# Attention, routed experts and a dense layer on one core: the routing's lists and re-ranking are issued a step at a time

## The chip, the core and the metric

One Trainium2 chip, one of its cores. The time is device microseconds of one execution of the whole program. Before the change three runs took 1547.67, 1550.4 and 1554.59 us; the median is 1550.4 us. A separate, profiled execution took 1545.65 us.

## What is computed

```python
# attention, per head: 32 packed queries p attend to k, v; then q attends to the packed result
p_packed = softmax(p k^T / 8) v
x = softmax(q p_packed^T / 8) p_packed            # 4608 tokens x 512
# routed experts: all 4608 x 8 scores in falling order
for idx in argsort(-(x @ w_gate).flatten()):
    tok, e = idx // 8, idx % 8
    if assigned[tok] >= 0 or counts[e] >= 576: continue
    assigned[tok] = e; counts[e] += 1
for e in range(8):
    out[assigned == e] = relu(x[assigned == e] @ w1[e]) @ w2[e]
# dense layer: 512 -> 2048 -> 512
h = out @ w_in;  result = (h * tanh(softplus(h))) @ w_out
```

Each expert ends with exactly 576 tokens.

## The kernel before

The program has three stretches. Attention comes first; its last part writes the token rows `x` to DRAM (`px`). Then the experts: for each, 192 products "up" (`pm<-xh,w` and `pm<-xl,w`, results `h`) and 192 "down" (`pm<-h,w`, results `y`), 288 columns each; a float32 product is made of three, of high and low parts of both sides. Then the dense layer (`ph`, `po`).

The routing (class `Routing`) runs beside the experts' products. It doesn't sort: it finds the experts one after the other in the order in which they fill up (0 to 7 here, in that order). For each, `search` finds the threshold score in seven digits. A digit is a chain: VectorE compares all tokens with the steps (`ge`, line 359), PE counts (line 367), VectorE copies the counts (`sb`, 372), PE adds them up (376), VectorE compares with the places left (`ind`, 380), PE spreads the answer (383), VectorE takes the digit over (`dg`, `at`, 387 to 390). `accept` marks the tokens of the found expert (`be`, `run`), re-ranks what is left (`rank`, lines 319 to 340: the best open score of each token as `m`, `ev`, `am`, `oh`, `key`, `first`), and PE counts places in line 435, called "total" here. `ids` then builds the expert's list of tokens on VectorE (`p0`, `pi`, `pif`, `oj`, `rj`, `oh`, lines 449 to 466), PE gathers it (470, 478), and `idx` is the list.

PE's order is written by hand. `Turns` counts one turn per product; a generator that yields n is resumed n turns later. The routing, the `fetch` of the next expert and the decoding of the dense layer's 64-bit weights (`Decode.step`, tiles `dt`, `dbig`) are such generators. How many turns each waits stands in the table `WAITS`, by expert 0, expert 1 and all later ones. The other engines' instructions are put in order by the scheduler; only those passed through `keep_in_program_order` stay in the written order against each other.

`fetch(k)` waits until expert k is found, loads the expert's number from `ei` on SyncE's queue, and asks for weights: each of eight loads is a DMA to `raw`, a cast on ScalarE (`w<-raw`, 513) and four subtractions of 256 columns on GpSimd (`w<-raw,w`, 516), here called splits. There are ten weight tiles, so those of the next expert come as the running one gives its tiles back. Then `gather` fetches the token rows on GpSimd's DMA queue (`xg`, 619), and PE transposes them (`pt`, 630) for `xh` (ScalarE) and `xl` (VectorE).

```python
    def __call__(self, n=1, idle=False):     # Turns: one call per product
        for s in list(self.streams):
            if idle and not s[2]: continue
            s[1] -= n
            while s[1] <= 0:
                wait = next(s[0], None)
```

Of the kernel before, what the change touches and what calls it, by code (L numbers as in the profile page):

```python
# [244 lines left out]
class Routing:  # L245
# [7 lines left out]
    def __init__(self, tc, a, consts, wk, ident, idx_all):  # L253
# [8 lines left out]
        self.code, self.pcode = rc[:, 128:136], rc[0:8, 136:137]  # L262
        self.tri = T([128, 128], BF, "tri")
# [55 lines left out]
    def rank(self):  # L319

        nc, V, T, L = self.nc, self.nc.vector, self.tile, self.L

        def bc(ap):
            return ap[:, :, None].to_broadcast([128, 36, NE])

        m = T([128, 36], F32, "m")
        V.tensor_reduce(m, L, axis=AX.X, op=OP.max)
        ev = T([128, 36, NE], F32, "ev", 1)
        V.tensor_tensor(ev, L, bc(m), op=OP.is_equal)
        key = self.key = T([128, 36], I32, "key")  # L330
        bits = m.bitcast(I32)
        V.tensor_scalar(key, bits, 31, -0x80000000, op0=OP.arith_shift_right, op1=OP.bitwise_or)
# [3 lines left out]
        V.tensor_mul(ev, ev, self.code[:, None, :].to_broadcast([128, 36, NE]))  # L336
        am = self.next_am = T([128, 36], F32, "am")
        V.tensor_reduce(am, ev, axis=AX.X, op=OP.max)
        self.oh = T([128, 36, NE], F16, "oh8", 1)
        V.tensor_tensor(self.oh, ev, bc(am), op=OP.is_equal)  # L340

    def search(self, k):
# [57 lines left out]
        V.tensor_scalar(self.ei[0:1, k:k + 1], a[0:1], -1.0, float(NE), op0=OP.mult, op1=OP.add)  # L400
        V.tensor_add(self.closed, self.closed, a)
        r = T([8, 3], F32, "r")
        V.scalar_tensor_tensor(sc[0:8, 0:n - 1], pc[0:8, 1:n], 1.0, dg[0:8, 0:n - 1], op0=OP.mult, op1=OP.mult,
                               accum_out=r[:, 0:1])
        V.tensor_tensor(r[:, 1:2], self.rem, r[:, 0:1], op=OP.subtract)
        V.tensor_scalar(r[:, 2:3], self.pcode, a[0:8], float(NT), op0=OP.is_equal, op1=OP.mult)
        V.tensor_tensor(self.rem, r[:, 1:2], r[:, 2:3], op=OP.max)
        cl = T([128, NE], F32, "cl")
        V.tensor_scalar(cl, self.code, a, -BIG, op0=OP.is_equal, op1=OP.mult)
        V.tensor_add(L, L, cl[:, None, :].to_broadcast([128, 36, NE]))  # L410

    def accept(self, k):
        nc, V, T, q = self.nc, self.nc.vector, self.tile, self.q
        t, a = q[:, 0:1], q[:, 1:2]
        z = T([128, 4, 36], F32, "z")
# [15 lines left out]
        if k < NE - 2:  # L431
            self.rank()
        yield wait(k, "total")
# [9 lines left out]
        self.slot = z[:, 2]  # L443

    def ids(self, k, slot):
        nc, V, T = self.nc, self.nc.vector, self.tile
        p0 = T([128, 36], I32, "p0", 1)
        self.tc.keep_in_program_order(
            V.tensor_scalar(p0, slot, 0.5, -32.0 * WIDE, op0=OP.is_lt, op1=OP.mult))
        V.scalar_tensor_tensor(p0, slot, 64.0 * (k % 2) - 1.0, p0, op0=OP.add, op1=OP.add)  # L450
        pi = T([128, 2, 36], I32, "pi", 1)
        V.tensor_scalar(pi[:, 1], p0, 5, None, op0=OP.arith_shift_right)
        V.tensor_scalar(pi[:, 0], p0, 31, None, op0=OP.bitwise_and)
        pif = T([128, 2, 36], BF, "pif", 1)
        V.tensor_copy(pif, pi)
# [4 lines left out]
        oj = T([128, 9, 20, 4], BF, "oj", 1)  # L460
        V.tensor_tensor(oj, spread(pif[:, 1], 20), self.steps[:, :, 0:20], op=OP.is_equal)
        rj = T([128, 2, 9, 20, 4], BF, "rj", 1)
        for h in range(2):
            V.tensor_tensor(rj[:, h], oj, spread(self.parts[:, h], 20), op=OP.mult)  # L464
        oh = T([128, 9, 32, 4], BF, "oh", 1)
        V.tensor_tensor(oh, spread(pif[:, 0], 32), self.steps[:, :, 0:32], op=OP.is_equal)
# [25 lines left out]
    def phases(self, turns):  # L492
        for k in range(NE):
            yield from self.search(k)
            self.found = k
            yield from self.accept(k)
            while k and k - 1 not in self.idx:
                yield 1
            turns.add(self.ids(k, self.slot))
# [265 lines left out]
def fused_kernel(ctx: ExitStack, tc: tile.TileContext, a: dict, out: bass.AP):  # L765
# [38 lines left out]
    with tc.manual_schedule(engines={mybir.EngineType.PE}):  # L804
# [12 lines left out]
        def fetch(k):  # L817
            while rt.found < k:
                yield 1
            w = ex.weights(k)  # L820
            for _ in range(4):
                next(w)
            while k not in rt.idx:
                yield 1
            yield from ex.gather(k, rt.idx[k], w)

        def decode():
            for i in range(32):
                yield DECODE - 6 * DECODE_OP
                yield from dec.step(words(i), i // 2, i % 2)  # L830
# [98 lines left out]
```

## Time and profile before

| what | before |
|---|---|
| median of 3 runs | 1550.4 us (1547.67 to 1554.59) |
| profiled execution: its time / its span | 1545.65 us / 1543.9 us |
| PE busy | 1447.7 us, 94% of the span |
| VectorE (DVE) / ScalarE (ACT) / GpSimd (POOL) busy | 821.6 / 783.2 / 417.9 us |
| first "up" product of expert 0, last "down" of expert 7 | 190.14, 741.72 us |

The profile has one page and a trace that answers questions. A view of windows gives each engine's busy time in a stretch, with the TensorE clock that was granted there as a share of 2.4 GHz. A view of waits names who waited for whom. A timeline lists instructions in order of time. Line numbers are those of the listing.

### The profile page before, as it was taken

What the parts mean: (1) busy time and instruction counts of PE and PEld (TensorE: products, weight loads), DVE (VectorE), ACT (ScalarE), POOL (GpSimd) and SP (SyncE); (2) the same over time, 40 slices, a digit from 0 to 9 for tenths busy, and PEclk for the clock granted to TensorE, in tenths of its full rate; (3) what the DMA queues carried; (4) which work ended last, traced back from release to release, by engine and by line L of the source; (5) the groups of instructions that cost most, each with busy time, mean ns of one, the idle gap of its engine ahead of it and who ended that gap; (6) DMA issues with size and microseconds to landing.
All of it is one profiled execution on the core that took longest, in us unless ns stands there. A gap on an engine that the chain in (4) does not pass through costs nothing.

```text
span 1543.9 us, 22783 instructions
## 1 busy us (share of the span) xinstructions
PE 1447.7 (94%) x9009; PEld 1195.1 (77%) x9009; DVE 821.6 (53%) x1632; ACT 783.2 (51%) x966; POOL 417.9 (27%) x572
## 2 busy tenths in 40 slices
PE   6879698898979899999999999999999999999997
PEld 3335487787879798999888888888888888888885
DVE  4765576757586776432344454444444444444443
ACT  2334443433333344544656565666656565656564
POOL 2441355546454647742601010010101000010101
PEclk9998798998989999999999999999999999999999
DMA  9743636345444556742502020100102010100000
GB/s 344 289 140 137 212 128 212 135 158 169 151 143 170 167 178 210 267 159 100 181 1 81 1 82 0 55 28 25 58 1 82 1 55 28 55 29 0 28 0 28
DMA packets 66843, 165.38 MB, mean 107 GB/s; under 512 B 8880, under 2 KB 21808, under 8 KB 66736
## 3 DMA queue, kind: packets, MB, share of 16 engines
q1 hardware_dynamic: 60656, 144.00, 27.1%
q0 software_dynamic: 6080, 19.93, 3.9%
q8 instruction: 71, 1.16, 0.3%
q14 instruction: 36, 0.29, 0.1%
HBM read 117.76 MB, written 46.14 MB: 106 GB/s over the span
## 4 chain that ended last, share of the span: by engine, by line
issue 48%; PE 32%; DVE 10%; POOL 5%; DMA 3%; ACT 1%; SPq 0%; POOLq 0%; ACTq 0%
PE pm L592 21%; PE px L238 3%; PE po L734 2%; PE ph L592 2%; POOL w L211 2%; POOL w L516 2%; POOL out L744 2%; DMA raw<-in_w 1%; PE pt L630 1%; DVE h L656 1%; DVE rj L464 1%; DVE w L180 1%; PE pr L376 1%; PE pr L367 1%; PE big L108 1%
## 5 line engine op out<-in xcount | busy, mean ns | idle before, releaser
L592 PE MATMUL ph<-y,w 128*128 128x512 f32 x1728 | 414.9, 395 | 0.0
L734 PE MATMUL po<-w,g 128*128 128x512 f32 x1728 | 410.1, 394 | 0.1
L592 PEld LDWEIGHTS ph<-y,w 128*128 128x128 f32 x1728 | 324.2, 188 | 78.1
L734 PEld LDWEIGHTS po<-w,g 128*128 128x128 f32 x1728 | 324.9, 188 | 74.6 <-ACT g L709 0.9
L709 ACT ACTIVATE u<-u 128x1024 f32<-128x1024 f32 (+1 forms) x219 | 229.4, 1049 | 194.4 <-DVE u L713 192.8
L516 POOL TENSOR_TENSOR w<-raw,w 128x256 fp32r<-128x256 f32 x320 | 248.2, 812 | 130.0 <-ACT w L513 92.3
L592 PE MATMUL pm<-h,w 128*128 128x288 f32 x1536 | 240.3, 307 | 1.4 <-DVE h L656 1.4
L592 PE MATMUL pm<-xh,w 128*128 128x288 f32 x1024 | 225.3, 309 | 13.6 <-DVE h L656 12.9
L744 POOL DMA_INDIRECT out<-ot,idx_all x36 | 35.0, 973 | 726.7 <-DVE ot L742 720.9
L592 PEld LDWEIGHTS pm<-h,w 128*128 128x128 f32 x1536 | 214.0, 193 | 6.2 <-DVE h L656 1.8
L713 DVE TENSOR_SCALAR u<-ph 128x1024 f32<-128x1024 f32 (+1 forms) x73 | 88.2, 1210 | 201.2 <-PE ph L592 201.2
L592 PEld LDWEIGHTS pm<-xh,w 128*128 128x128 f32 x1024 | 173.5, 196 | 17.4 <-DVE h L656 14.3
L709 ACT ACT_TABLE_LOAD x144 | 184.8, 1283 | 2.5
L716 DVE TENSOR_TENSOR u<-ph,u 128x1024 f32<-128x1024 f32 (+1 forms) x73 | 88.2, 1210 | 172.6 <-ACT u L709 172.6
L592 PE MATMUL pm<-xl,w 128*128 128x288 f32 x512 | 157.7, 308 | 0.1
L709 ACT ACTIVATE g<-u 128x1024 fp32r<-128x1024 f32 (+1 forms) x73 | 76.4, 1048 | 101.3 <-DVE u L718 101.3
L718 DVE TENSOR_TENSOR u<-ph,u 128x1024 f32<-128x1024 f32 (+1 forms) x73 | 88.1, 1208 | 73.2 <-ACT u L709 73.2
L513 ACT ACTIVATE w<-raw 128x1024 fp32r<-128x1024 f32 x80 | 84.1, 1056 | 62.9 <-DMA raw<-in_w 45.7
L655 ACT ACTIVATE h<-pm 128x288 fp32r<-128x288 f32 x128 | 51.5, 408 | 118.1 <-PE pm L592 117.9
L592 PEld LDWEIGHTS pm<-xl,w 128*128 128x128 f32 x512 | 100.5, 196 | 1.4 <-DVE xl L633 0.5
L720 DVE TENSOR_TENSOR g<-u,g 128x1024 fp32r<-128x1024 f32 (+1 forms) x73 | 87.8, 1204 | 2.3 <-ACT g L709 2.3
L656 DVE SCALAR_TENSOR_TENSOR h<-pm,h 128x288 fp32r<-128x288 f32 x128 | 56.9, 449 | 48.3 <-ACT h L655 47.8
(157 smaller groups left out, 1140.3 us busy)
## 6 DMA issues: line engine op xcount, KB each, us to landing
raw<-in_w SPq DMA_DIRECT2D x64, 512.0 KB, 3.7
yd<-y SPq DMA_DIRECT2D x64, 288.0 KB, 2.7
kt<-in_k SPq DMA_DIRECT2D x16, 576.0 KB, 8.3
qt<-in_q SPq DMA_DIRECT2D x16, 576.0 KB, 7.4
vt<-in_v SPq DMA_DIRECT2D x16, 512.0 KB, 6.4
xd<-xt SPq DMA_DIRECT2D x32, 256.0 KB, 2.0
draw<-in_win SPq DMA_DIRECT2D x16, 512.0 KB, 4.4
wd<-dbig SPq DMA_DIRECT2D x32, 256.0 KB, 2.6
```

What stands on the lines that cost most here:

```text
L513: nc.scalar.activation(w[:, 0].rearrange("p a b -> p (a b)"), raw, AF.Copy)
L516: op = nc.gpsimd.tensor_sub(lo[:, c:c + PIECE], raw[:, c:c + PIECE], hi[:, c:c + PIECE].bitcast(F32))
L592: nc.tensor.matmul(out, l, r, start=i == 0 and m == 0, stop=i == n - 1 and m == 2)
L655: nc.scalar.activation(h[:, 0], ph, AF.Relu)
L656: nc.vector.scalar_tensor_tensor(h[:, 1], ph, 0.0, h[:, 0].bitcast(F32), op0=OP.max, op1=OP.subtract)
L709: op = nc.scalar.activation(*args, **kw)
L713: for step in (lambda p: V.tensor_scalar(u[:, p], ph[:, p], 20.0, None, op0=OP.min), lambda p: A(u[:, p], u[:, p], AF.Exp), lambda p: A(u[ ...
L716: lambda p: V.tensor_tensor(u[:, p], ph[:, p], u[:, p], op=OP.max),
L718: lambda p: V.tensor_mul(u[:, p], ph[:, p], u[:, p]),
L720: lambda p: V.tensor_sub(gt[:, 1, p], u[:, p], gt[:, 0, p].bitcast(F32))):
L734: self.nc.tensor.matmul(self.po[m], gt[:, p, i, 128 * m:128 * m + 128], self.cw[8 + f // 2][:, q, f % 2], start=f == 0 and p == q == 0, st ...
L744: st = nc.gpsimd.indirect_dma_start(out=self.out, out_offset=bass.IndirectOffsetOnAxis(ap=self.idx_all[:, c:c + 1], axis=0), in_=ot, in_of ...
```

## The change

Four things, none of which alters the results.
- `rank` and `ids` become generators whose VectorE instructions are held in program order. A list instruction is issued every 1, 4 or 7 turns (`list`, for expert 0, 1 and later), a re-ranking step every 2, 3 or 4 (`op`). Closing the found expert and re-ranking come as `close`, six steps of it before "total".
- The waits get shorter: `start`, `count`, `pick`, `total` and `ids`; "total" waits 8, 18 or 24 turns instead of 12, 38 or 48.
- `ev` and `am` become bf16 tiles.
- `found` is set after these steps, and the next expert's weights and rows are asked for 0, 10 or 60 turns later (`fetch`); decoding has 75 turns instead of 85, and none of its units begins while `border` is set, from accepting until the list is under way.

```diff
-WAITS = dict(start=(22, 10, 24), count=(4, 14, 22), pick=(1, 6, 13), any=(1, 6, 6), total=(12, 38, 48),
-             ids=(20, 54, 92), rows=(29, 50, 54), row=(6, 14, 19))
-DECODE, DECODE_OP, LOAD = 85, 7, 40
+WAITS = dict(start=(20, 6, 20), count=(4, 14, 21), pick=(1, 6, 12), any=(1, 6, 6), total=(8, 18, 24),
+             op=(2, 3, 4), list=(1, 4, 7), ids=(12, 20, 30), rows=(29, 50, 54), row=(6, 14, 19), fetch=(0, 10, 60))
+DECODE, DECODE_OP, LOAD = 75, 7, 40
...
+    def close(self, k, a):
+        V, T, pin, r = self.nc.vector, self.tile, self.tc.keep_in_program_order, self.r
+        cl = T([128, NE], F32, "cl")
+        pin(V.tensor_scalar(cl, self.code, a, -BIG, op0=OP.is_equal, op1=OP.mult))
+        pin(V.tensor_add(self.L, self.L, cl[:, None, :].to_broadcast([128, 36, NE])))
+        yield
+        yield from self.rank()
+        pin(V.tensor_tensor(r[:, 1:2], self.rem, r[:, 0:1], op=OP.subtract))
...
-        if k < NE - 2:
-            self.rank()
-        yield wait(k, "total")
+        steps = self.close(k, a) if k < NE - 2 else iter(())
+        left = wait(k, "total")
+        while k and left >= wait(k, "op"):
+            next(steps, None)
+            left -= wait(k, "op")
+            yield wait(k, "op")
...
+        self.found = k
+        yield left
         pq = self.psum()
         nc.tensor.matmul(pq[:, 0:72], self.tri, bef, start=True, stop=False)
...
+        while k and k - 1 not in self.idx:
+            yield 1
+        turns.add(self.ids(k, z[:, 2]))
+        for _ in steps:
+            yield wait(k, "op")
+        self.border = False
...
+        for op in (lambda: V.tensor_scalar(p0, slot, 0.5, -32.0 * WIDE, op0=OP.is_lt, op1=OP.mult),
...
+                   lambda: V.tensor_tensor(oh, spread(pif[:, 0], 32), self.steps[:, :, 0:32], op=OP.is_equal)):
+            pin(op())
+            yield wait(k, "list")
         yield wait(k, "ids")
...
             while rt.found < k:
                 yield 1
+            yield wait(k, "fetch")
             w = ex.weights(k)
...
                 yield DECODE - 6 * DECODE_OP
+                while rt.border:
+                    yield 1
                 yield from dec.step(words(i), i // 2, i % 2)
```

How it moves instructions, at three places. PE, "total" of expert 5 (lines 435 and 436, now 456 and 457); the rows around it are products. Before:

```order
L592 MATMUL pm<-xl,w 128x288
L592 MATMUL pm<-xh,w 128x288
L435 LDWEIGHTS tri
L435 MATMUL pr<-be,tri 128x72
L436 LDWEIGHTS onesb
L436 MATMUL pr<-run,onesb 128x72
L592 MATMUL pm<-xh,w 128x288
```

Now:

```order
L616 MATMUL pm<-h_1_5590,w 128x288 x3
L616 MATMUL pm<-h_1_5694,w 128x288 x2
L456 LDWEIGHTS tri
L456 MATMUL pr<-be,tri 128x72
L457 LDWEIGHTS onesb
L457 MATMUL pr<-run,onesb 128x72
L616 MATMUL pm<-h_1_5694,w 128x288
L616 MATMUL pm<-h_1_5768,w 128x288 x3
```

It stood in "up" of expert 4 (`xh`, `xl`) and stands now in "down" of expert 3 (`h`), 181 products earlier.

ScalarE, the weights of expert 5 and what stands around their casts (line 513, now 537). Before, in "up" of expert 4:

```order
L655 ACTIVATE h_1_6548<-pm 128x288
L547 ACTIVATE dbig<-dbig,tiny 128x512
L513 ACTIVATE w<-raw 128x1024
L655 ACTIVATE h_0_6566<-pm 128x288
L513 ACTIVATE w<-raw 128x1024
L655 ACTIVATE h_1_6614<-pm 128x288
L549 ACTIVATE dbig<-dbig 128x512
L513 ACTIVATE w<-raw 128x1024
```

Now, at the end of "down" of expert 3; the two casts in one row are the last ones of expert 4:

```order
L691 ACTIVATE y<-pm 128x288
L656 ACTIVATE xh<-pt 128x4x128
L571 ACTIVATE dbig<-dbig,tiny 128x512
L573 ACTIVATE dbig<-dbig 128x512
L537 ACTIVATE w<-raw 128x1024 x2
L569 ACTIVATE dbig<-draw 128x512
L656 ACTIVATE xh<-pt 128x4x128
L691 ACTIVATE y<-pm 128x288
L537 ACTIVATE w<-raw 128x1024
L679 ACTIVATE h_0_6671<-pm 128x288
```

The first cast of expert 5 is the last `w` row: it has moved 48 products up, and its "total" 181. The last set of transposed rows (`xh`) stands behind two casts now.

VectorE, the list of expert 2. Before:

```order
L656 SCALAR_TENSOR_TENSOR h_1_3761<-pm,h_1_3761 128x288
L452 TENSOR_SCALAR pi<-p_3712 128x36
L453 TENSOR_SCALAR pi<-p_3712 128x36
L315 TENSOR_SCALAR digit<-key 128x36
L455 CAST pif<-pi 128x72
L461 TENSOR_TENSOR oj<-pif,steps 128x720
L466 TENSOR_TENSOR oh<-pif,steps 128x1152
L464 TENSOR_TENSOR rj<-oj,parts 128x720 x2
L656 SCALAR_TENSOR_TENSOR h_0_3782<-pm,h_0_3782 128x288
```

Now, the second half of that list:

```order
L488 CAST pif<-pi 128x72
L318 TENSOR_SCALAR digit<-key 128x36
L572 SCALAR_TENSOR_TENSOR dt<-draw,dt 128x512
L489 TENSOR_TENSOR oj<-pif,steps 128x720
L680 SCALAR_TENSOR_TENSOR h_0_3733<-pm,h_0_3733 128x288
L490 TENSOR_TENSOR rj<-oj,parts 128x720
L491 TENSOR_TENSOR rj<-oj,parts 128x720
L388 TENSOR_SCALAR ind<-pr,rem 8x32
L574 SCALAR_TENSOR_TENSOR dt<-draw,dt 128x512
L492 TENSOR_TENSOR oh<-pif,steps 128x1152
L680 SCALAR_TENSOR_TENSOR h_1_3763<-pm,h_1_3763 128x288
```

The products' `h` and the search's `ind` stand between the list's instructions.

## Rows read from the trace of the kernel before

**Rows 1.** Windows, two experts: length, busy time per engine (instructions), PEclk, DMA share, GB/s

```profile
345.50:417.90 72.40, 65.61 (x559) 60.02 (x558) 48.97 (x147) 28.19 (x51) 40.19 (x50) 0.93 0.51 164
626.60:679.70 53.10, 53.10 (x406) 53.10 (x405) 24.95 (x41) 27.52 (x51) 31.19 (x44) 1.00 0.60 213
```

**Rows 2.** Waits of PE, 190 to 745 us: in total, times, longest

```profile
PE pr L376 <- DVE sb L372: 19.2, 5, 6.8
PE pm L592 <- DVE h L656: 14.3, 8, 5.6
PE pr L470 <- DVE rj L464: 6.7, 1, 6.7
```

**Rows 3.** Windows: six stretches of waiting and low clock (engines: PE, PEld, DVE, ACT, POOL)

```profile
233.20:247.80 14.60, 7.88 (x70) 6.97 (x71) 10.65 (x25) 5.12 (x8) 10.61 (x13) 0.53 0.62 198
303.40:316.10 12.70, 5.88 (x27) 5.51 (x27) 10.28 (x21) 4.01 (x6) 6.96 (x9) 0.60 0.53 177
310.30:316.10 5.80, 5.80 (x26) 5.42 (x26) 3.42 (x11) 0.95 (x2) 1.42 (x2) 0.50 0.31 102
371.60:384.30 12.70, 6.07 (x28) 5.70 (x28) 10.14 (x23) 2.98 (x6) 9.19 (x10) 0.60 0.61 188
442.00:456.00 14.00, 8.06 (x34) 7.42 (x35) 10.40 (x22) 2.76 (x5) 5.88 (x7) 0.63 0.43 144
513.30:524.30 11.00, 6.11 (x28) 5.73 (x29) 7.58 (x19) 1.79 (x5) 6.93 (x9) 0.69 0.62 207
579.00:585.70 6.70, 3.06 (x13) 3.05 (x13) 6.67 (x12) 3.02 (x4) 6.70 (x8) 0.75 0.49 157
```

**Rows 4.** Groups by line, GpSimd, 294.3 to 309 us: busy, mean ns

```profile
L516 POOL TENSOR_TENSOR w<-raw,w 128x256 fp32r<-128x256 f32 x16 | 13.2, 861 | 12.9 <-ACT w L513 12.9
L555 POOL TENSOR_TENSOR dbig<-dt,dbig 128x256 f32<-128x256 f32 x2 | 1.4, 742 | 0.0
```

**Rows 5.** Timeline of VectorE, list of expert 2: start, duration

```profile
297.67 0.77 DVE L315 TENSOR_SCALAR digit<-key 128x36 int32<-128x36 int32 x1
...
299.07 1.33 DVE L359 TENSOR_TENSOR ge<-at,steps 128x1152 f16<-128x1152 bf16 x1
...
305.20 0.98 DVE L461 TENSOR_TENSOR oj<-pif,steps 128x720 bf16<-128x720 bf16 x1
306.11 1.28 DVE L466 TENSOR_TENSOR oh<-pif,steps 128x1152 bf16<-128x1152 bf16 x1
307.31 2.02 DVE L464 TENSOR_TENSOR rj<-oj,parts 128x720 bf16<-128x720 bf16 x2
```

**Rows 6.** Timeline of VectorE, list of expert 0

```profile
171.88 0.75 DVE L359 TENSOR_TENSOR ge<-at,steps 128x1152 f16<-128x1152 bf16 x1
...
172.77 0.18 DVE L315 TENSOR_SCALAR digit<-key 128x36 int32<-128x36 int32 x1
...
173.63 0.53 DVE L461 TENSOR_TENSOR oj<-pif,steps 128x720 bf16<-128x720 bf16 x1
174.08 0.75 DVE L466 TENSOR_TENSOR oh<-pif,steps 128x1152 bf16<-128x1152 bf16 x1
174.75 0.97 DVE L464 TENSOR_TENSOR rj<-oj,parts 128x720 bf16<-128x720 bf16 x2
```

**Rows 7.** Timeline: last product of the search and `run`, experts 2 and 4

```profile
287.26 0.18 PE L383 MATMUL pr<-ind,which 8*128 8x17 f16 x1
290.61 0.29 DVE L430 TENSOR_TENSOR_SCAN run<-onesb,be 128x72 bf16<-128x72 bf16 x1
424.80 0.18 PE L383 MATMUL pr<-ind,which 8*128 8x17 f16 x1
430.91 0.29 DVE L430 TENSOR_TENSOR_SCAN run<-onesb,be 128x72 bf16<-128x72 bf16 x1
```

**Rows 8.** Timeline: last set of transposes for expert 2, and its `xl`

```profile
343.15 0.66 PE L630 MATMUL pt<-ident,xg 128*128 128x128 f32 x4
344.48 0.69 DVE L633 TENSOR_TENSOR xl<-pt,xh 128x512 fp32r<-128x512 f32 x1 [0.18 <-ACT xh L632]
```

**Rows 9.** Costliest groups of the page: the low parts of "up"

```profile
L656 DVE SCALAR_TENSOR_TENSOR h<-pm,h 128x288 fp32r<-128x288 f32 x128 | 56.9, 449 | 48.3 <-ACT h L655 47.8
```

More of the change, by code (lines that the diff above doesn't have):

```diff
@@ L262, in __init__ @@
         self.code, self.pcode = rc[:, 128:136], rc[0:8, 136:137]
+        self.codeb = T([128, NE], BF, "codeb")
+        P.tensor_copy(self.codeb, self.code)
         self.tri = T([128, 128], BF, "tri")
@@ L310, in load @@
                                   pt[:, 96 * i:96 * i + 96].rearrange("p (r q e) -> p r q e", r=3, q=4))
-        self.rank()
+        for _ in self.rank():
+            pass
     def digit(self, i):
@@ L319, in rank @@
     def rank(self):
-        nc, V, T, L = self.nc, self.nc.vector, self.tile, self.L
+        V, T, L, pin = self.nc.vector, self.tile, self.L, self.tc.keep_in_program_order
         def bc(ap):
@@ L399, in search, with accept @@
         self.at = at
-        V.tensor_scalar(self.ei[0:1, k:k + 1], a[0:1], -1.0, float(NE), op0=OP.mult, op1=OP.add)
-        V.tensor_add(self.closed, self.closed, a)
-        r = T([8, 3], F32, "r")
+        r = self.r = T([8, 3], F32, "r")
         V.scalar_tensor_tensor(sc[0:8, 0:n - 1], pc[0:8, 1:n], 1.0, dg[0:8, 0:n - 1], op0=OP.mult, op1=OP.mult,
                                accum_out=r[:, 0:1])
-        V.tensor_tensor(r[:, 1:2], self.rem, r[:, 0:1], op=OP.subtract)
+    def close(self, k, a):
[3 more added lines that the diff above has]
+        pin(V.tensor_add(self.L, self.L, cl[:, None, :].to_broadcast([128, 36, NE])))
+        yield
+        yield from self.rank()
+        pin(V.tensor_tensor(r[:, 1:2], self.rem, r[:, 0:1], op=OP.subtract))
         V.tensor_scalar(r[:, 2:3], self.pcode, a[0:8], float(NT), op0=OP.is_equal, op1=OP.mult)
         V.tensor_tensor(self.rem, r[:, 1:2], r[:, 2:3], op=OP.max)
[L408 to L412, printed above, removed]
+    def accept(self, k, turns):
         nc, V, T, q = self.nc, self.nc.vector, self.tile, self.q
         t, a = q[:, 0:1], q[:, 1:2]
+        self.border = True
         z = T([128, 4, 36], F32, "z")
@@ L430, in accept @@
         V.tensor_tensor_scan(run, self.onesb[:, 0:72], bef, 0.0, op0=OP.mult, op1=OP.add)
-        if k < NE - 2:
-            self.rank()
-        yield wait(k, "total")
+        steps = self.close(k, a) if k < NE - 2 else iter(())
[4 more added lines that the diff above has]
+            yield wait(k, "op")
+        if k < NE - 1:
+            V.tensor_add(self.closed, self.closed, a)
+            V.tensor_scalar(self.ei[0:1, k:k + 1], a[0:1], -1.0, float(NE), op0=OP.mult, op1=OP.add)
+        self.found = k
+        yield left
         pq = self.psum()
@@ L442, in accept @@
         V.tensor_add(z[:, 2], z[:, 2], z[:, 3])
-        self.slot = z[:, 2]
+        while k and k - 1 not in self.idx:
[4 more added lines that the diff above has]
+        self.border = False
     def ids(self, k, slot):
         nc, V, T = self.nc, self.nc.vector, self.tile
+        pin = self.tc.keep_in_program_order
         p0 = T([128, 36], I32, "p0", 1)
-        self.tc.keep_in_program_order(
-            V.tensor_scalar(p0, slot, 0.5, -32.0 * WIDE, op0=OP.is_lt, op1=OP.mult))
@@ L450, in ids @@
-        V.scalar_tensor_tensor(p0, slot, 64.0 * (k % 2) - 1.0, p0, op0=OP.add, op1=OP.add)
         pi = T([128, 2, 36], I32, "pi", 1)
-        V.tensor_scalar(pi[:, 1], p0, 5, None, op0=OP.arith_shift_right)
-        V.tensor_scalar(pi[:, 0], p0, 31, None, op0=OP.bitwise_and)
         pif = T([128, 2, 36], BF, "pif", 1)
-        V.tensor_copy(pif, pi)
+        oj = T([128, 9, 20, 4], BF, "oj", 1)
+        rj = T([128, 2, 9, 20, 4], BF, "rj", 1)
+        oh = T([128, 9, 32, 4], BF, "oh", 1)
         def spread(v, n):
@@ L458, in spread @@
             return v.rearrange("p (g c) -> p g c", c=4)[:, :, None, :].to_broadcast([128, 9, n, 4])
[L460 to L466, printed above, removed]
+        for op in (lambda: V.tensor_scalar(p0, slot, 0.5, -32.0 * WIDE, op0=OP.is_lt, op1=OP.mult),
+                   lambda: V.scalar_tensor_tensor(p0, slot, 64.0 * (k % 2) - 1.0, p0, op0=OP.add, op1=OP.add),
+                   lambda: V.tensor_scalar(pi[:, 1], p0, 5, None, op0=OP.arith_shift_right),
+                   lambda: V.tensor_scalar(pi[:, 0], p0, 31, None, op0=OP.bitwise_and),
+                   lambda: V.tensor_copy(pif, pi),
+                   lambda: V.tensor_tensor(oj, spread(pif[:, 1], 20), self.steps[:, :, 0:20], op=OP.is_equal),
+                   lambda: V.tensor_tensor(rj[:, 0], oj, spread(self.parts[:, 0], 20), op=OP.mult),
+                   lambda: V.tensor_tensor(rj[:, 1], oj, spread(self.parts[:, 1], 20), op=OP.mult),
+                   lambda: V.tensor_tensor(oh, spread(pif[:, 0], 32), self.steps[:, :, 0:32], op=OP.is_equal)):
+            pin(op())
+            yield wait(k, "list")
@@ L494, in phases @@
             yield from self.search(k)
[L495 to L499, printed above, removed]
+            yield from self.accept(k, turns)
 class Weights:
```

22 lines of the change are left out of this document (13 added, 9 removed).

## The prediction

> **What bounds it now.** I read the page first: PE is busy for 94% of the span, so only stretches in which it waits or runs at its lower clock can give time back. The windows by expert show where. An expert whose products run beside the routing takes 72.4 us at a mean granted clock of 0.93; one whose products run after the routing is over takes 53.1 us at 1.00 [rows 1]. The difference is the routing's own products plus waits. The list of PE's waits says that the waits are for VectorE: 19.2 us for `sb`, 14.3 us for `h`, 6.7 us for `rj`, 40.2 us in all [rows 2]. ACT and DMA end almost none.
>
> Six stretches hold most of it, one behind each of the routing's "total" products of experts 1 to 6 (I number experts from 0 in the order in which routing finds them). Each is an idle PE and then a PE at granted clock 0.50, that is 1.2 instead of 2.4 GHz [rows 3]. From each row: idle is length less PE busy, and what PE was busy for ran at half speed, so half of that is lost too. That gives 6.7 + 3.9, 6.8 + 2.9, 6.6 + 3.0, 5.9 + 4.0, 4.9 + 3.1 and 3.6 + 1.5: losses of 10.7, 9.8, 9.7, 10.0, 8.0 and 5.2 us, **53 us** together. Some 5.6 us of small waits (40.2 less 34.6) lie between them.
>
> Why is VectorE late? Take the second stretch. In the 14.7 us from 294.3 to 309 GpSimd is busy for 14.6, 13.2 of them with weight splits (line 516) [rows 4], and in just these us VectorE's small instructions are longer than in list 0, where GpSimd stands idle: `digit` 0.77 us against 0.18, `ge` 1.33 against 0.75, `oj` 0.98 against 0.53, `oh` 1.28 against 0.75, the two `rj` 2.02 against 0.97 [rows 5, 6]. That is 0.59 + 0.58 + 0.45 + 0.53 + 1.05 = 3.2 us; ten more small ones of the accepting, the list and the search (`asg`, `at`, `z`, `up`, `digit`, `p` twice, `pi` twice, `pif`) are of `digit`'s kind and lose from nothing to its 0.59, at 0.45 each 4.5. So the stretching is an estimated 7.7 us and the idle time 6.8: without the splits in that place there would be no wait. The list's last instructions stand in one lump ahead of the next `h`, and PE needs both `sb` and `h`.
>
> **The change, part by part.** Base: the profiled execution, 1545.65 us (span 1543.9); the three runs' median is 1550.4, so I add 4.75 at the end.
>
> *Where the list now falls against the splits.* The routing's turns for one expert go from 359 to 317 (count 7, pick 7, start 4, total 24: 42 less), so from expert to expert the lists come 42 turns earlier, while the splits can't come earlier by as much: they need the weight tiles that the running expert's products give back. In ScalarE's order the first cast of an expert's weights stood 5 to 21 turns ahead of the "total" product for experts 1 to 6; now it stands 22 to 29 turns behind it for experts 1 to 4, and some 115 and 158 turns behind it for 5 and 6, past the whole list. Hence:
> - lists 5 and 6: no split beside them. Their 8.0 + 5.2 = 13.2 us go.
> - list 4: one cast beside it and the next one 60 turns later. One cast is split in four pieces, 4 x 0.86 = 3.4 us of GpSimd [rows 4], which can stretch four or five instructions, too little to make PE wait by the account above. I leave 1.5 of 10.0: 8.5 go.
> - lists 1 to 3: splits still come, but after accepting and the first three list instructions instead of before. Of list 2's 7.7 us of stretching, `asg`, `at`, `z`, `p` twice and one `digit` get free, about 3; some 4.7 stay. What stays is spread: a list instruction every 7 turns (4 for expert 1) with an `h` in between, so that PE's `h` is not behind a lump. I take **half**: 15 of 30.2.
> - the small waits, 5.6: half, 2.8.
>
> Together 13.2 + 8.5 + 15.1 + 2.8 = 39.6 us.
>
> *The waiting for "total" shrinks from 48 turns to 24.* A turn is 72.4 less list 3's 9.7, over 384: 0.163 us, so 24 turns are 3.9 us. From the last product of the search to `run`, which "total" needs, the row of the clean case has 287.26 to 290.90, 3.6 us, with ten instructions of closing and re-ranking in between, which now stand behind `run`; in a case with splits 424.80 to 431.20, 6.4 us [rows 7]. In the new ScalarE order only list 3 has splits there (the last two of the expert before). Cost: 6.4 - 3.9 = 2.5 at most, nothing at least; I take 2.
>
> *The next expert's weights and tokens 60 turns later.* The casts of w1 hardly move in ScalarE's order, since the tiles bind them. The gathered rows' transposes do: the fifth set stood 15 to 63 turns ahead of the next expert's products, and now 3 turns (experts 2 to 7), so 15 ahead of the first product that reads it, 15 x 0.138 = 2.1 us (53.1 / 384). From transposes to `xl` the row has 343.15 to 345.17, 2.0 us [rows 8], and a weight cast now stands ahead of that `xh`. The gathers themselves get 60 turns more on GpSimd's queue, so they cost nothing. Late by nothing to 1.1 us; I take 0.5 six times, 3.
>
> *Priced at nothing.* bf16 in re-ranking: two of its products shrink from a few tenths; covered by VectorE's queue, counted in "half". `ei` and `closed` written later: SyncE's load of `ei` waits a few us more, but the weights queued behind it wait for tiles anyway; were that cover gone, a weight tile would be late, and PE would show a wait for ACT `w`, which it has none of now. Decoding steps every 75 turns instead of 85, but none begins while accepting and listing run: more work outside, less inside. List 0 (before any product): 10 turns instead of 4, and re-ranking now interleaved: -2 to +2, taken as 0.
>
> **Sum:** 39.6 - 2 - 3 = 34.6, so 1545.65 - 35 = 1510.6 on the profiled execution and **1515 us** on the median.
>
> GpSimd's total of splits per expert is the same before and after, so the stretching could simply hit other instructions. These would be the search's `ge`, `up`, `digit` and `at`. One step of the search with splits beside it then has 1.33 + 3 x 0.77 = 3.6 us of them, with three `h` of 0.45 [rows 9] 5.0 us, and its three reads of PSUM (`sb`, `ind`, `dg`), of `digit`'s clean size or a little over, make 5.6, against 39 turns or 6.3 us of PE: it fits. That is why I count the splits' new place as free. The Trainium skill says in "SBUF — State Buffer", Who interferes with whom, that a VectorE instruction with two SBUF inputs, or in a two-port mode, and a GpSimd one hold the shared ports for a whole instruction, and that the second to come fully blocks; by it alone the blocking is kept in sum wherever the splits go, the time would be near the rival "moves along" below, 1542, and the trace agrees in so far as the stretched durations are near a GpSimd piece's.
>
> **Rivals.**
> *The stretching moves along* (also: the change doesn't do what its words say, since casts keep their place in the first half). Lists 1 to 4 keep their 40.2, lists 5 and 6 lose half of their 13.2 to the search's steps, small waits stay; 6.6 saved, list 3 and the late transposes cost up to 2 + 3 (each of the latter 0.5). Net about -2 to -8: 1542 to 1548. For it: GpSimd's work is unchanged and VectorE is the late one. Against it: the search step fits, and the slots of lists 5 and 6 are clear.
> *All lists come clean.* 53.2 + 5.6 less 5: 1550.4 - 54 = 1496. For it: spacing and re-ranking apart might cover the 4.7 us that stay. Against it: list 1 has only 4 turns a step, lists 2 and 3 meet three or four splits.
> *"Total" becomes the wait* (slower). If GpSimd is at work between the search's last product and "total" for most experts, `run` takes 6.4 us against 3.9: 2.5 idle, and with the half clock behind it (0.4 to 0.7 us lost for each idle one [rows 3]) 4 us, six times 24. With the 53 of today kept, as the list is only as late as before, and late transposes at 1.1 x 6: 53 + 24 + 7 - 59 for a case in which lists 5 and 6 too meet splits = +25: 1575. It decides from three experts on; below that the saved lists pay for it. Against it: the order shows one such expert.
>
> **How the numbers follow.** A measurement can tell about 0.5%, 8 us, from no change. My forecast has 0.60, "all clean" 0.16, "moves along" 0.15, "total" 0.09. The range leaves out half of the slowest and a little of the fastest: 1493 to 1546. Faster by over 0.5% (under 1542.6) are the forecast, "all clean" and a fifth of "moves along": 0.79; within 0.5%: the rest of that, 0.12; slower: 0.09.
>
> **What will show it.** Right: PE's waits for `sb`, `rj` and `h` together under 20 us; the stretches behind the fifth and sixth "total" with no idle over 1 us and the clock at 1.00; `oj`, `rj` and `oh` of the fifth and sixth lists at 0.53, 0.49 and 0.75 us, those of the second and third still near 1; the windows of experts 3 and 4 near 62 us, ten less than expert 2 now [rows 1]. Small new waits of `pm` for `xl`. Wrong: waits of the "total" product for `run`; long `oj` in all six lists; or six stretches of half clock still there.

## The result and the profile after

The changed kernel takes **1537.3 us** (median of 5 runs, 1534.4 to 1541.7) where the kernel before takes 1550.9 in the runs beside it: a ratio of 0.991, interval 0.9884 to 0.9935. It is faster, inside the forecast's range, but by 13.6 us and not by 35. The profiled execution took 1535.47 us, its span is 1533.7.

| what | before | after |
|---|---|---|
| profiled execution: time / span | 1545.65 / 1543.9 us | 1535.47 / 1533.7 us |
| PE busy | 1447.7 us | 1442.2 us |
| VectorE / ScalarE / GpSimd busy | 821.6 / 783.2 / 417.9 us | 805.7 / 781.7 / 418.0 us |
| first "up" product of expert 0, last "down" of expert 7 | 190.14, 741.72 us | 188.45, 731.55 us |

The same windows as in [rows 1], expert 2 and expert 6 of the changed kernel:

```profile
349.75:420.95 71.20, 65.83 (x557) 59.94 (x556) 55.20 (x190) 29.28 (x53) 37.09 (x45) 0.95 0.51 172
614.65:669.52 54.87, 54.01 (x407) 53.23 (x405) 21.45 (x41) 26.09 (x49) 32.73 (x42) 1.00 0.61 204
```

Expert 2 is 1.2 us shorter than before; experts 3 and 4, which the forecast wanted near 62 us, take 73.0 and 66.5. GpSimd is as busy as before over the whole program. PE's waits from 188 to 745 us, which answer to [rows 2], have changed their names:

```profile
PE pr L375 <- DVE ge L367: 12.0, 6, 4.2
PE pr L391 <- DVE ind L388: 6.6, 4, 2.6
PE pr L498 <- DVE oh L492: 6.4, 1, 6.4
PE pr L384 <- DVE sb L380: 6.1, 5, 4.1
PE pm L616 <- DVE xl L657: 2.1, 1, 2.1
```

These are 33 us, against 40 in [rows 2]. `sb`, `rj` and `h` together have 6.9 of them, under the 20 that were to show the forecast right; as a sign this failed, because the waits went to other tiles. What was a wait for the list (`h` and `sb` behind its lump) is now mostly a wait for the search (`ge`, `ind`, `sb`). Where they lie is read from windows of PE alone (length, busy, granted clock, DMA), first the lists of experts 1 to 6, which answer to [rows 3], each from the start of its first wait to the end of the low clock:

```profile
228.80:247.00 18.20, 9.89 (x94) 0.72 0.60 205
293.30:304.90 11.60, 7.66 (x53) 0.85 0.58 198
362.60:373.20 10.60, 7.51 (x43) 0.68 0.42 140
422.90:424.30 1.40, 0.23 (x3) 1.00 0.85 266
481.90:482.80 0.90, 0.16 (x2) 1.00 0.93 364
532.60:546.00 13.40, 13.32 (x135) 1.00 0.24 90
```

The last three are almost clean: idle times of 1.2, 0.7 and 0.1 us, and the clock stays at 1.00 (2.4 GHz). The first three still hold idle times of 8.3, 3.9 and 3.1 us. PE ran at 0.50 in them from 236.6, 301.4 and 366.3 us on; that is half the clock, so an estimated half of what PE worked there is lost: 3.3, 1.7 and 3.1 us. Lists 1 to 6 lose 11.6 + 5.7 + 6.2 + 1.2 + 0.7 + 0.1 = **25.5 us**, where the kernel before lost 53. Then six stretches that had no wait of this length before. Four lie in the middle of a search; the third is a wait for a transpose's `xl`, and the last comes when the routing is over:

```profile
199.10:209.40 10.30, 8.15 (x53) 0.67 0.01 6
321.20:328.80 7.60, 3.50 (x18) 0.78 0.53 181
351.60:353.80 2.20, 0.10 (x2) 1.00 0.35 133
434.60:444.90 10.30, 7.16 (x41) 0.67 0.68 231
507.30:516.60 9.30, 5.14 (x32) 0.63 0.52 170
634.50:635.50 1.00, 0.17 (x2) 1.00 0.82 225
```

Idle 2.2 + 4.1 + 2.1 + 3.1 + 4.2 + 0.8 = 16.5 us, and at low clock, reckoned in the same way, 3.4, 1.7, 3.1 and 2.6 more: **27.3 us**. This is what the forecast lacks.

Two of these stretches show how it comes about. The one at 321 us, VectorE and then GpSimd in order of time (start, duration):

```profile
316.71 0.74 DVE L367 TENSOR_TENSOR ge<-at,steps 128x1116 f16<-128x1116 bf16 x1
317.37 7.14 DVE L371 SCALAR_TENSOR_TENSOR up<-digit,at 128x36 f32<-128x36 int32 x1
...
325.01 0.27 DVE L380 CAST sb<-pr 128x124 f16<-128x124 f32 x1
```

```profile
316.59 0.95 POOL L643 DMA_INDIRECT xg<-xd,idx  x1 [0.30 <-DVE dg L395]
317.56 2.80 POOL L540 TENSOR_TENSOR w<-raw,w 128x256 fp32r<-128x256 f32 x4
320.33 1.41 POOL L579 TENSOR_TENSOR dbig<-dt,dbig 128x256 f32<-128x256 f32 x2
321.70 2.75 POOL L540 TENSOR_TENSOR w<-raw,w 128x256 fp32r<-128x256 f32 x4
```

An `up` that takes 0.19 us alone takes 7.14: it ends when GpSimd's ten pieces, which follow each other without a gap, are over. The `sb` behind it comes 4.1 us too late for PE. The one at 507 us is of another kind; ScalarE, and then VectorE:

```profile
509.26 1.06 ACT L537 ACTIVATE w<-raw 128x1024 fp32r<-128x1024 f32 x1 [6.11 <-DMA raw<-in_w]
510.22 0.39 ACT L679 ACTIVATE h<-pm 128x288 fp32r<-128x288 f32 x1
```

```profile
510.64 0.46 DVE L680 SCALAR_TENSOR_TENSOR h<-pm,h 128x288 fp32r<-128x288 f32 x1 [5.33 <-ACT h L679]
511.02 0.43 DVE L367 TENSOR_TENSOR ge<-at,steps 128x540 f16<-128x540 bf16 x1
```

ScalarE stands for 6.11 us at a weight cast whose raw weight has not landed. The `h` behind it is late, VectorE's own `h` waits for that one, and `ge`, which PE wants, stands behind VectorE's `h`. The raw weight is late because of GpSimd, and twice over. The three raw tiles go round, and the one it needs came free with a split that ended at 502.24 us; then its load stood until 504.18 us behind a store of decoded weights (`wd<-dbig`) in SyncE's queue, which waited for GpSimd's `dbig` until 503.65. It landed at 509.24.

The stretch at 434 us has the same rows on ScalarE and VectorE, with 5.17 us; there the load stood for its tile alone, until 429.73 us. The one at 199 us is a mixture: 1.85 us of such a wait, then an `at` of 0.70 us and a `ge` of 1.21, each behind a piece.

### The profile page after: what moved, and what is told of

It is laid out like the page before. It is cut to its first block, busy times and chain, and to the rows that moved or that the text cites. A ratio compares the mean times of both kernels' runs of the same rounds, so it can differ in the third digit from the quotient of the medians.

```text
span 1533.7 us, 22792 instructions
## 1 busy us (share of the span) xinstructions
PE 1442.2 (94%) x9009; PEld 1191.5 (78%) x9009; DVE 805.7 (53%) x1627; ACT 781.7 (51%) x966; POOL 418.0 (27%) x573
## 4 chain that ended last, share of the span: by engine, by line
issue 46%; PE 33%; DVE 10%; POOL 6%; DMA 3%; ACT 1%; SPq 0%; POOLq 0%; DVEq 0%; ACTq 0%
PE pm L616 21%; PE ph L616 3%; PE po L758 3%; PE px L238 3%; POOL w L211 2%; POOL out L768 2%; POOL w L540 2%; DMA raw<-in_w 2%; PE pt L654 1%; DMA kt<-in_k 1%; DVE up L371 1%; DVE h L680 1%; DVE r L185 1%; POOL xg L643 1%; DVE r L197 1%
## 5 line engine op out<-in xcount | busy, mean ns | idle before, releaser
L616 PE MATMUL pm<-h,w 128*128 128x288 f32 x1536 | 233.7, 304 | 0.0
```

What stands on the lines that cost most here:

```text
L616: nc.tensor.matmul(out, l, r, start=i == 0 and m == 0, stop=i == n - 1 and m == 2)
```

## The experiments

Each median has the kernel before beside it on the same chip: 1550.3 us for the first run without splits, the delay, the turns of before and the casts held; 1553.5 for the steps in one go, the casts further apart, the piece of 512 and the changed kernel's splits on VectorE; 1554.4 for the two runs that ask which of the two it is and for the last run; 1551.2 for the others. Between groups the ratios compare better than the times. The profiles of these kernels differ by up to 6.5 us at the start alone: the first "up" product stands between 187.8 and 194.3 us, with a wait of up to 7.1 us for the first gather.

**Splits left out.**

```diff
-            op = nc.gpsimd.tensor_sub(lo[:, c:c + PIECE], raw[:, c:c + PIECE], hi[:, c:c + PIECE].bitcast(F32))
+            op = nc.gpsimd.memset(lo[:, c:c + PIECE].bitcast(F32), 0.0)
```

> This kernel leaves out the low halves of all the split weights: GpSimd writes zeros there in place of the subtraction, and reads no SBUF. After's losses (idle PE plus half clock between the first and the last product of the experts) are 54.6 us. Theory 'splits': what holds VectorE up in the search and in lists 1 to 3 is GpSimd's subtraction beside it; then the losses fall below 12 us, the experts beside routing take under 65 us, and the time is 1490 to 1500. Theory 'density': a search of 317 turns is simply too tight for its chain of instructions; then the waits for ge stay (6 of them, about 12 us and as much half clock) and the time stays above 1525.

Measured 1503.7 us (0.9703, interval 0.9641 to 0.9766): 3.7 us above the range of 'splits' and over 20 below that of 'density'. The longest wait left beside the routing is one of 4.1 us for `ge`, at 234 us. The same edit in the kernel before:

> The kernel before the change, with the low halves of all split weights left out (GpSimd writes zeros in place of the subtraction). My account of before says that without the splits beside the lists there would be no wait: its six stretches (53 us) and small waits (6 us) go, 1490 to 1505, and the change has nothing left to gain (the changed kernel without splits came to 1504). Rival: the lump of list instructions delays h by itself; half of the 53 us stays and the time is 1515 to 1530.

Measured 1502.5 us (0.9684, interval 0.9645 to 0.9723), inside its range. The windows of expert 2 (PE alone), in the changed kernel and in the one before, both without splits:

```profile
338.39:402.55 64.16, 63.12 (x558) 1.00 0.57 192
```

```profile
335.43:399.15 63.72, 63.08 (x559) 1.00 0.55 187
```

So what I read from before holds: without the splits its lists have next to no wait, but for one of 3.2 us behind list 1. The splits cost the changed kernel 34 us and the one before 49. Take them away, and the change has nothing to gain. This edit also frees the raw weights sooner, so it doesn't tell the two kinds of stretch apart. For the lists of before the trace does. While PE stood for list 2, VectorE worked for 6.87 of 6.90 us (third of the five busy times) and stood for none of ScalarE's `h`; the other five stretches are alike:

```profile
303.40:310.30 6.90, 0.08 (x2) 0.09 (x2) 6.87 (x11) 3.06 (x5) 5.54 (x7) 0.68 0.71 240
```

**The delay of 60 turns undone.** Edit: `fetch=(0, 10, 60)` becomes `fetch=(0, 0, 0)`.

> The next weights and tokens are asked for without the 60 turns of delay, all else as in the changed kernel. Theory 'the delay matters' (it keeps splits and late casts away from lists): lists 4 to 6 lose again some 10 us and the time is 1546 to 1552. Theory 'the tiles bind the casts': the casts stand within 30 turns of where they are in the changed kernel, and the time is within 3 us of its 1537; the one wait of a product for xl (2.1 us) is gone.

Measured 1534.6 us (0.9927, interval 0.9894 to 0.996; the change itself 0.991). The delay does nothing that the runs can tell, as the theory 'the tiles bind the casts' has it. The wait for `xl` is gone, as expected.

**The turns of before.** Edit: `start`, `count`, `pick` and `total` of `WAITS` as before; the steps stay apart.

> Routing's start, count, pick and total waits are put back to those of the kernel before (359 turns for each expert), and the list's and re-ranking's steps stay apart as in the change. Theory 'earlier lists': the gain of lists 4 to 6 (21 us) comes from lists that now fall ahead of the splits; put back, these lists meet the splits again, the waits for ge in the search are gone, and the time is 1543 to 1552. Rival 'steps apart': issuing the list a step at a time is what saves the lists; then they stay clean, the search gets its room back, and the time is 1510 to 1528.

Measured 1540.5 us (0.9948, interval 0.9914 to 0.9982), between the two. The waits behind lists 4 to 6 are 3.5, 2.6 and 1.3 us: more than in the changed kernel, less than before (5.6, 4.9 and 3.6). So both parts of the change help a list. But the search of these longer turns has its row waits as well:

```profile
195.63 10.44 DVE L398 TENSOR_SCALAR at<-up,dd 128x36 bf16<-128x36 f32 x1
335.08 6.24 DVE L398 TENSOR_SCALAR at<-up,dd 128x36 bf16<-128x36 f32 x1
```

PE waits 9.5 and 3.8 us behind these two. The theory 'density' of the first run falls with them: such waits come in the longer search too.

**The steps in one go.** The opposite: turns as changed, but the steps of `close` all before "total" and the list's nine without a turn between them (experts 1 to 7).

```diff
+        if k:
+            for _ in steps:
+                pass
...
             pin(op())
-            yield wait(k, "list")
+            if k == 0:
+                yield wait(k, "list")
```

> The changed kernel with its turns (317 for each expert) and casts, but for experts 1 to 7 the list's nine instructions and the closing and re-ranking are each issued in one go, as before. My prediction's account (where the list falls against the splits is what gains): lists 4 to 6 stay clean, lists 1 to 3 lose some 5 us more each at most, 1537 to 1550. Rival, after the run with the turns of before, which kept the small list waits and came to 1540: issuing the steps apart is what gains; then waits for h and sb behind each list come back and the time is 1548 to 1560.

Measured 1545.1 us (0.9955, interval 0.9918 to 0.9992): in the range of my account, and no different from the turns of before within the intervals; the change's own interval overlaps too. Lists 5 and 6 stay nearly clean (0.9 us of wait behind the fifth, none behind the sixth), so it is the turns that cleaned them; behind lists 2 and 3 single waits of 3.6 and 4.6 us are back. This run too has waits for a row: one `at` of 10.2 us, two `up` of 7.0 and 7.1.

**Casts held.** The casts of the next expert's weights keep the program's order, the first six 24 turns apart.

```diff
+        cast = nc.scalar.activation(w[:, 0].rearrange("p a b -> p (a b)"), raw, AF.Copy)
+        if hold:
+            hold(cast)
...
+        def spaced(w):
+            for _ in range(6):
+                next(w)
+                yield SPACE
```

> ScalarE's casts of the next expert's first six weights are held where the program writes them, one every 24 turns from the moment that the expert is found, in place of where the scheduler hoists them. Theory 'ScalarE in order': the waits for ge at 437 and 511 us come from an h that stands behind a cast whose raw weight has not landed; with the casts held later, the raws are there, these two waits (6.7 us and 5.6 of half clock) go, and lists 1 to 3 meet at most one cast: 1510 to 1528. Rival 'ports': the same splits stretch whatever VectorE does then, and the time stays within 8 us of 1537; or, with casts held later, a weight comes late and products wait for w: slower than 1540.

Measured 1531.4 us (0.9889, interval 0.9833 to 0.9945), six less than the change and not the 10 to 27 of the theory; the interval holds the change's 0.991, so the six are not shown. ScalarE's group of casts from 188 to 745 us, first of the changed kernel, then of this one (count, busy, mean, idle before):

```profile
L537 ACT ACTIVATE w<-raw 128x1024 fp32r<-128x1024 f32 x72 | 74.9, 1055 | 51.6 <-DMA raw<-in_w 39.2 <-DMA raw<-wd 11.4 <-POOL w L540 0.5
```

```profile
L538 ACT ACTIVATE w<-raw 128x1024 fp32r<-128x1024 f32 x73 | 76.6, 1054 | 17.8 <-DMA raw<-wd 13.1 <-DMA raw<-in_w 4.7
```

The waiting for raw weights of the experts fell from 39.2 to 4.7 us, and the waits for `ge` at 437 and 511 us went. Three new ones for `sb` came, 6.0, 6.8 and 4.5 us, behind these:

```profile
244.31 9.88 DVE L372 SCALAR_TENSOR_TENSOR up<-digit,at 128x36 f32<-128x36 int32 x1
...
314.31 9.88 DVE L372 SCALAR_TENSOR_TENSOR up<-digit,at 128x36 f32<-128x36 int32 x1
...
497.99 7.24 DVE L372 SCALAR_TENSOR_TENSOR up<-digit,at 128x36 f32<-128x36 int32 x1
```

Both theories hold for their own waits: with the raw weights there in time, GpSimd has more pieces in a row, and one wait takes the other's place.

**Casts further apart.** Edit: `SPACE = 40`.

> As the run with held casts, but one cast every 40 turns instead of 24. Theory 'starvation' (a VectorE instruction such as up or at, once it waits for GpSimd, waits until GpSimd's unbroken row of instructions ends, 7 to 10 us): with casts further apart GpSimd's rows are shorter, so at most one VectorE instruction over 4 us is left of that run's three, and the time is 1508 to 1526. Rival: the lengths of these rows come from the gathers ahead of them and not from the spacing; three long ones stay, and the time is 1527 to 1537; or the last casts come late and products wait for w, over 1537.

Measured 1535.7 us (0.9879, interval 0.9837 to 0.992). The rival has it: three `up` remain that take 7.1, 7.1 and 9.9 us. Each begins as a gather's issue on GpSimd (`xg`, 0.95 us) ends, and behind the five issues of a gather a row of 10 to 14 pieces follows without a gap, at either spacing.

**Size of a piece.** Edit: `PIECE = 512`, and in another kernel `PIECE = 128`.

> GpSimd's splits and decoding products in pieces of 512 instead of 256: twice as long each, half as many, the same rows of work. Theory 'a piece': what costs is that an instruction of VectorE waits for the end of one piece; digit, up, at beside it go from 0.72 to about 1.3 us, and the losses between the first and the last product (54.6 us) grow by 15 to 30 us: 1550 to 1568. Theory 'a whole row': the cost sits in the few instructions that wait for all the pieces of a row, and the time stays within 8 us of 1537.

> The changed kernel with pieces of 128 columns instead of 256 on GpSimd. By the row 512: 1562, 256: 1537, no splits: 1504, a shorter piece stretches each VectorE instruction less; if GpSimd's instruction shrinks from 0.72 to about 0.4 us, digit, up and at beside it take about 0.42, and the time is 1518 to 1530. Rival: the number of instructions costs GpSimd so much more time that its rows get longer: 1535 to 1545.

Measured 1562.4 us (1.0064, interval 1.0039 to 1.0088) with 512 and 1579.7 us (1.0203, interval 1.0166 to 1.0239) with 128. So 256 is the best of the three. With 512 the theory 'a piece' has its number; with 128 neither expectation has. The instruction `up` and GpSimd's split (minimum/median/maximum in ns, first and last start) with 512:

```profile
L371 DVE SCALAR_TENSOR_TENSOR up<-digit,at x34: 175/190/6435, 198.8 to 540.1; 128x36 f32<-128x36 int32 x34
L540 POOL TENSOR_TENSOR w<-raw,w x136: 1251/1288/1925, 188.2 to 718.4; 128x512 fp32r<-128x512 f32 x136
```

and with 128 the split, and VectorE at the worst place:

```profile
L540 POOL TENSOR_TENSOR w<-raw,w x530: 442/457/1163, 187.9 to 718.8; 128x128 fp32r<-128x128 f32 x177
```

```profile
518.96 14.54 DVE L318 TENSOR_SCALAR digit<-key 128x36 int32<-128x36 int32 x1
519.81 13.69 DVE L680 SCALAR_TENSOR_TENSOR h<-pm,h 128x288 fp32r<-128x288 f32 x1
520.56 12.95 DVE L380 CAST sb<-pr 128x124 f16<-128x124 f32 x1
```

A piece of 512 stretches most `up` and half of the `digit` beside GpSimd to between 1.1 and 1.3 us instead of 0.72, as the theory says. A piece of 128 takes 457 ns and not half of 736, so that a row of 24 pieces, three weights, takes 9.90 us where 8 pieces of 256, two weights, take 5.5. The rows get longer: one `digit` waits for 14.5 us and holds up `h` and `sb` behind it, which read PSUM. PE stands for 11.3 us there.

**Splits on VectorE.** For experts 1 to 7, the changed kernel:

```diff
+    def steps(self, src, out, pin):
...
+        pin(nc.scalar.activation(hi, raw, AF.Copy))
+        yield 10
+        for c in range(0, 1024, PIECE):
+            pin(nc.vector.tensor_sub(lo[:, c:c + PIECE], raw[:, c:c + PIECE], hi[:, c:c + PIECE].bitcast(F32)))
+            yield 4
+        yield SPACE - 26
```

> The splits of the weights of experts 1 to 7 are done by VectorE (32 pieces of 256 for each expert, 4 turns apart, 10 turns behind their cast) and not by GpSimd. Theory 'ports': the long instructions of the search (over 1.7 us) and the stretched ones are gone, VectorE gains some 37 us of busy time from the first to the last product (after against the run without splits) and pays 56 weights x 4 x 0.35 = 78 us, of which about 50 in the experts beside routing; it has 15 us free in each of these, so the time is 1505 to 1525. Rival 'VectorE is simply full': its instructions wait for one another instead, and the time is over 1537.

Measured 1518.5 us (0.9757, interval 0.9712 to 0.9801), 19 less than the change and inside the range of 'ports'. A piece costs VectorE 443 ns where the expectation had 350, and GpSimd needed 0.74 us for it. The edit does a second thing: it also holds the casts in program order, 32 turns apart, from the moment that the expert is found. How much of the 19 us that gives is not tried by itself; in the run with casts held above it gave nothing that the runs can tell. The same in the kernel before:

> The kernel before the change, with the splits of experts 1 to 7 on VectorE, held in program order as in the run of the changed kernel that came to 1518. If the change's gain is only that its lists and steps suffer less from GpSimd, this comes out beside it, 1512 to 1525. If steps issued apart help by themselves (VectorE is now fuller), the lump is worse here: 1530 to 1545.

Measured **1498.2 us** (0.9654, interval 0.9608 to 0.97): below its expectation, 20 us less than the changed kernel with the same splits (16 by the ratios, whose intervals don't meet), and no run here is faster. PE's waits from 210 to 745 us, first of the kernel before, then of the changed one (ahead of 210 us each has one of over 7 us for `ge`, behind a long `at`):

```profile
PE pr L384 <- DVE ind L381: 0.9, 3, 0.4
PE pm L608 <- DVE h L677: 0.6, 2, 0.3
PE pr L471 <- DVE rj L465: 0.6, 1, 0.6
PE pr L377 <- DVE sb L373: 0.3, 1, 0.3
```

```profile
PE pr L392 <- DVE ind L389: 6.0, 7, 1.6
PE pr L385 <- DVE sb L381: 5.6, 3, 2.4
PE pr L376 <- DVE ge L368: 3.2, 5, 1.4
PE pr L499 <- DVE oh L493: 0.5, 1, 0.5
```

Without GpSimd in the way, the change costs time. Most of its waits stand 41 to 59 turns behind each "total" product, where its list of 63 turns and the next search, begun 4 turns sooner, share VectorE. Two runs ask which of the two it is. First the turns of before, the steps still apart:

> The changed kernel with splits on VectorE (1518.5), and routing's start, count, pick and total waits of the kernel before (359 turns for each expert). Theory 'the 42 turns cost': with a list of 63 turns and a search that now starts 4 turns sooner and runs 38 turns less, the first steps of the search stand behind the list in VectorE's order (waits for sb and ind 53 to 59 turns behind each total product); with the turns of before these go and the time is 1496 to 1505, as the kernel before with the same splits (1498). Theory 'steps apart cost': 1512 to 1520.

Measured 1510.2 us (0.9718, interval 0.9681 to 0.9755), between the two expectations. Then the steps in one go, the turns as changed:

> The changed kernel with splits on VectorE, its 317 turns kept, but the list's nine instructions and the re-ranking issued in one go for experts 1 to 7. Theory 'the 42 turns cost': the search is still as tight, 1514 to 1525. Theory 'steps apart cost' (a list spread over 63 turns lies across the next search's first steps): 1496 to 1506.

Measured 1520.1 us (0.9785, interval 0.9749 to 0.9821). This is in the range of 'the 42 turns cost'. So of the 20 us the 42 turns cost an estimated 8 (6 by the ratios, whose intervals overlap) and the steps apart nothing that shows. The other 12 stay open. In the profiles the largest part lies in the window of expert 0, 86.2 us with the turns of before against 79.7 in the kernel before: PE waits 4.2 us for list 1 there, and VectorE stood 2.25 us at a decoding step (`dt`) whose raw weight had not landed, just ahead of `oj`.

Two more versions. The changed kernel with the last four weights of expert 0 on VectorE as well, and no split while `border` is set:

> As the changed kernel with splits on VectorE (1518.5), and besides: the last four weights of expert 0 are split there too, and splits wait while accepting, closing and re-ranking run. Expected: the wait of at for GpSimd in list 0's search (7.4 us of idle PE and as much again at half clock) goes, and the waits for sb and ind beside lists 3 to 5 (10 us, and 10 of half clock) shrink by half: 1500 to 1510. If it is VectorE's fullness that makes those, 1514 to 1522.

Measured 1507.4 us (0.9727, interval 0.9694 to 0.9761), in the expected range, but only half for its reason: the wait behind a long `at` in list 0's search went, while the waits of over 0.7 us for `sb` and `ind` behind lists 3 to 5 stay, 7.9 us against 9.3. By the ratios it is 5 us ahead of 1518.5, inside the noise. The kernel before with these four on VectorE too:

> The kernel before with the splits of experts 1 to 7 on VectorE (1498), and the last four weights of expert 0 split there too. If the one wait left there (7.25 us for ge at 205 us, behind an at of 7.99 us that waits for 12 instructions of GpSimd) goes with GpSimd's splits, with its half clock 8 to 13 us are saved: 1485 to 1491. If the at waits for something else, or four more splits on VectorE delay the first search as much: 1495 to 1500.

Measured 1499.5 us (0.9653, interval 0.9616 to 0.9689), no less than 1498.2. No long `at` is left and the wait of 7.25 us for `ge` went, so that one was GpSimd's. But a wait of 2.7 us for `sb` came in its place, so that expert 0's window is only 2.1 us shorter; those of experts 1 to 4 are 2.9 us longer together, and the first "up" product came at 192.2 us instead of 187.8. The time stays.

## Why the prediction was half right

*What bounds it* holds, and the two runs without splits and VectorE's unbroken work in the six stretches show it: the lists were late because of the splits beside them.

*Lists 4 to 6.* Predicted: 21.7 of 23.2 us go, 1.5 stay. Measured: 2.0 stay. The run with the steps in one go shows that it is the turns which clean lists 5 and 6, as the forecast had it; `rj` of list 5 is still 1.06 us, twice its clean time, beside a decoding product (`dbig`) on GpSimd, and makes no wait of a microsecond.

*Lists 1 to 3.* Predicted: half of 30.2 stays, 15.1 us. Measured: 23.5. List 1 gained nothing (11.6 against 10.7). It is the splits beside it, fifteen without a gap, and not its steps of only 4 turns: with casts held GpSimd has four there, the steps are the same, and PE's wait for its `oh` fell from 6.4 to 0.9 us. The `oh` of list 1, first in the changed kernel, then with casts held:

```profile
238.96 1.27 DVE L492 TENSOR_TENSOR oh<-pif,steps 128x1152 bf16<-128x1152 bf16 x1
```

```profile
234.51 0.75 DVE L493 TENSOR_TENSOR oh<-pif,steps 128x1152 bf16<-128x1152 bf16 x1
```

Lists 2 and 3 kept 5.7 and 6.2 us of 9.8 and 9.7, a little more than the half that was forecast.

*"Total" and the transposes.* Priced at 2 and 3 us; measured nothing and 2.1 (one of six transposes was late, by its `xl` at 353.7 us).

*The search.* The step that failed is "That is why I count the splits' new place as free". It added up one stretched instruction after another, 5.6 us, and compared that with 39 turns, 6.3 us. Measured in its place: 27.3 us less the 2.1 of the transposes, 25.2 us (0.8 of it behind the routing). With the 8.4 more of lists 1 to 3 and 0.5 of lists 4 to 6, less what was priced too high (2.8 of small waits, 2 of "total", 0.9 of transposes) and a first product 1.7 us earlier, that makes 26.7; the profiled execution missed by 24.9 (1535.5 against 1510.6). The account missed two things. An instruction doesn't always wait for one piece but at times for GpSimd's whole row: 7.14 us at 317. That the wait may last a whole instruction, as the Trainium skill says in "SBUF — State Buffer", Who interferes with whom, is the common case here (0.72 us); the trace shows more than that. And the queue behind the splits was left out: the raw tiles come free by GpSimd, so a cast waits for its weight, and ScalarE's and VectorE's `h` and the search's `ge` stand behind the cast (5.17 and 6.11 us). The second is the larger: the stretches at 434 and 507 us lose 6.2 and 6.8 us, the one at 321 us 5.8. No row of the first stood in the profile of before, where the longest `up` of the search was 0.73 us and the longest `at` 0.92; a sum of means could not find it. The second did stand there and wasn't read: ScalarE's casts waited 40.7 us for raw weights from 188 to 745 us, about as long as after (39.2), only that no `ge` stood long behind them:

```profile
L513 ACT ACTIVATE w<-raw 128x1024 fp32r<-128x1024 f32 x70 | 73.5, 1056 | 48.2 <-DMA raw<-in_w 40.7 <-DMA raw<-wd 5.7 <-PE pm L592 1.5
```

*The rivals.* "The stretching moves along" was closest in mechanism, only that lists 4 to 6 were saved and the search paid; its 1542 to 1548 and the forecast's 1515 lie on either side of 1537. "Total becomes the wait" did not happen, nor did "all lists come clean": lists 1 to 3 keep 23.5 us.

## What to carry to other kernels

GpSimd's splits found no free place beside the chains of small VectorE instructions here: when such work is moved away from one chain, ask which chain it meets next, and price that with the longest wait a row of it can make, not with the mean. Ask also what stands behind the engines that wait for it; the profile's own row of the casts showed that wait. Before spending a change on where two engines meet, leave the work of one of them out for one run; here that run gave 1503 us for both schedules and suggested giving the work to another engine. The version that came of it, the schedule of before with the splits on VectorE and the casts held, takes 1498 us.

## What was not expected of the hardware

- VectorE's small SBUF instructions beside GpSimd mostly get in behind one piece (0.72 us of 256 columns, about 1.27 of 512), but some wait until GpSimd's unbroken row is over: 7.14 us for 10 pieces, 9.88 in the run with casts held, 14.54 us for 34 pieces of 128 columns. Many of these began just as a gather's issue on GpSimd ended; some did not, and what decides it stays open.
- GpSimd's subtraction took 457, 736 and 1288 ns for 128, 256 and 512 columns: an estimated 0.18 us of each piece is there whatever its size (twice 457 less 736, and twice 736 less 1288).
- Instructions that read PSUM were not stretched beside the splits: `sb` took 0.20 to 0.29 us there in the changed kernel. They were late only behind one that was.
- With zeros written in place of the splits, `up`, which reads two tensors of SBUF, kept its 0.18 to 0.19 us in the three cases that fell beside them. The Trainium skill says the same in "SBUF — State Buffer", Who interferes with whom: an instruction with two SBUF inputs meets only GpSimd instructions that read SBUF. `at`, which reads one tensor, did wait beside a row of zeros, 4.4 us at most.
